# Two relus of batch 1 one chunk later on VectorE, and the last row tile cut as 384 and 128 columns, in a fused linear attention and mixer kernel

## Chip, cores, metric

One core of a Trainium2 chip. The metric is the device time of one launch in microseconds; differences below 1% matter here, so every comparison is between runs of both kernels in the same rounds on the same chip. A profile is one such launch, so it has the scatter of one.

## The reference

Eight batches, 8 heads, 576 positions, head size 64. Linear attention with phi(x) = elu(x) + 1, then a mixer: an MLP over positions (576 to 256 to 576), a residual, an MLP over channels (512 to 1536 to 512), a residual.

```python
q_p, k_p = phi(q), phi(k)
kv  = einsum('bhsd,bhse->bhde', k_p, v);  z = sum(k_p, axis=2)
x   = einsum('bhsd,bhde->bhse', q_p, kv) / (einsum('bhsd,bhd->bhs', q_p, z) + 1e-6)   # heads joined: 512
u   = x + (relu(x.T @ w_tok1) @ w_tok2).T      # mm1, mm2
out = u + relu(u @ w_ch1) @ w_ch2              # mm3, mm4
```

## The kernel before

Everything is in SBUF; the batches are pipelined by hand. A `big` list holds the steps of mm3 and mm4, and after step i the small work of later batches that is listed for i is issued. The order within each engine is the order of issue. The parts that the argument touches (cuts marked `...`):

```python
ps_big = ctx.enter_context(tc.tile_pool(name="ps_big", bufs=4, space=bass.MemoryType.PSUM))
...
def mm3(n, mc, kjs=range(NDM), dve=False):           # chunk mc of 12: 128 hidden channels x 512 positions
    if kjs[0] == 0:
        part_of[mc] = ps_big.tile([128, 512], FP32, name="c_ps", tag="big")
    ...                                              # 4 matmuls (L475)
    if kjs[-1] == NDM - 1 and dve:                   # relu and cast to bf16: VectorE (L479) ...
        nc.vector.tensor_scalar(out=cr[b][:, mc, :], in0=ps, scalar1=0.0, scalar2=None, op0=ALU.max)
    elif kjs[-1] == NDM - 1:                         # ... or ScalarE (L482)
        nc.scalar.activation(out=cr[b][:, mc, :], in_=ps, func=AF.Relu)

def utr_tail_dma(p):                                 # the 9th rows of two batches, transposed by DMA (L464)
    nc.sync.dma_start_transpose(out=uTt, in_=ut[p % 2])

def mm4_last(c):                                     # last row tile of the last batch, in two halves
    p, b, r, cs = B // 2 - 1, 1, R - 1, COLS[c]
    ...                                              # 12 matmuls (L537), add of u on VectorE (L540)
    for e in range(2):
        (nc.scalar if e else nc.sync).dma_start(out=outv[2 * p + b, :, 2 * r + e, cs], in_=o[half[e]])
...
# batch 1: chunks 3..11, then mm3 of the tail rows (three steps), then mm4; phi of k of batch 2 at steps 0 and 2
big = [... mm3(1, mc, range(2, 4)) for mc in range(3)] + [... mm3(1, mc, dve=mc in (4, 7)) for mc in range(3, NCH)] + m3t + ...
fill = [(s, lambda g=g: phi("k", 2, g)) for g, s in ((0, 0), (1, 2))]
fill += [(4, lambda: vcast(2, 0)), (5, lambda: vcast(2, 1, nc.vector.tensor_copy))]
...
# batch 2 (n == 2, d == 1), all on the queue of SyncE: transposes, loads of batch 5, then the tail transpose at step 15
fill += [(12 + d, lambda: qtr_dma(n + 2))]
if n == 2:
    fill += [(12 + d, lambda: load_all(5, "qkv"))]
```

The kernel starts with 27 `warm` matmuls (`warm(27)`) that only keep TensorE busy until the first loads are in.

## Time and profile before

| | |
|---|---|
| time | 266.18 us median of 3 (265.37 to 266.49) |
| span of the profiled run | 264.5 us |
| TensorE busy | 97% |
| last group of matmuls starts, ends | 257.87, 260.65 us |
| from the start of that group to the end of the span | 6.6 us |

With TensorE busy nearly throughout, a time difference must show as a difference in where TensorE stands. A matmul of 512 columns is drawn 0.38 us long but the next one starts 0.216 us later, so up to 0.16 us of standing still can hide between two bars: steps from start to start are the safe measure.

### The profile page before, as it was taken

The numbers are of one execution on the slowest core, as the hardware profiler recorded it, in microseconds if no ns is written. First come the engines' busy times: TensorE is split into PE (matmuls) and PEld (weight loads), VectorE is DVE, ScalarE is ACT, GpSimd is POOL, SyncE is SP. The second block draws the span as 40 slices with busy tenths as digits, with TensorE's granted clock in tenths as the row PEclk, the third lists the DMA queues.
The fourth block names the chain that finished last, engine by engine and source line by source line (L and its number), as shares of the span: only waits on it lengthen the run. The fifth ranks groups of instructions, "written<-read, shape, count | busy, mean of one in ns | idle before, by whom it ended". The sixth has DMA issues, their size and how long they took to land.

```text
span 264.5 us, 5173 instructions
## 1 busy us (share of the span) xinstructions
PE 255.8 (97%) x2119; PEld 135.0 (51%) x2119; DVE 158.3 (60%) x312; ACT 132.8 (50%) x200; POOL 33.0 (12%) x54
## 2 busy tenths in 40 slices
PE   7899999999999999999999999999999999999994
PEld 3585445554744454445564554445554554444643
DVE  5764977966839886948684296938684272420122
ACT  4644878268456358525771358425870354027300
POOL 9720300020002300030001300030001300000000
PEclk9999999999999999999999999999999999999999
DMA  7999999499405997799999991671065500740043
GB/s 249 251 203 276 377 210 400 150 182 402 183 2 105 185 330 283 93 234 347 323 412 216 247 408 54 143 163 45 2 120 131 119 2 0 144 114 2 0 98 101
DMA packets 50087, 48.34 MB, mean 183 GB/s; under 512 B 30288, under 2 KB 35536, under 8 KB 50064
## 3 DMA queue, kind: packets, MB, share of 16 engines
q1 hardware_dynamic: 41904, 35.53, 46.5%
q0 software_dynamic: 7440, 11.44, 20.7%
q10 hardware_dynamic: 720, 1.05, 1.3%
q8 instruction: 16, 0.26, 0.4%
q14 instruction: 7, 0.06, 0.1%
HBM read 35.85 MB, written 9.44 MB: 171 GB/s over the span
## 4 chain that ended last, share of the span: by engine, by line
PE 87%; DVE 5%; DMA 3%; ACT 2%; POOL 1%; issue 1%; ACTq 0%; POOLq 0%
PE h_ps L501 34%; PE c_ps L475 27%; PE a_ps L248 6%; PE h_ps L261 5%; PE c_ps L489 4%; PE nd_ps L210 3%; DMA cr<-in_v_dram 3%; PE kv_ps L169 2%; DVE y L131 1%; PE h_ps L537 1%; DVE cr L479 1%; DVE kp L140 1%; PE bank L363 1%; PE bank L413 1%; DVE e L139 1%
## 5 line engine op out<-in xcount | busy, mean ns | idle before, releaser
L475 PE MATMUL c_ps<-uT,wc 128*128 128x512 bf16 x384 | 91.4, 379 | 0.8 <-ACT uT L444 0.4
L482 ACT ACTIVATE cr<-c_ps 128x512 bf16<-128x512 f32 x91 | 53.5, 599 | 77.1 <-PE c_ps L475 76.9
L501 PE MATMUL h_ps<-wc,cr 128*128 128x512 bf16 x372 | 84.9, 379 | 0.0
L501 PEld LDWEIGHTS <-cr 128*128 128x128 bf16 x372 | 36.0, 98 | 41.3
L475 PEld LDWEIGHTS <-wc 128*128 128x128 bf16 x384 | 35.8, 98 | 37.2 <-issue 1.7
L518 DVE TENSOR_TENSOR o_sb<-h_ps,u 128x512 f32<-128x512 f32 x31 | 21.1, 688 | 23.1 <-PE h_ps L501 23.0
L523 POOL DMA_DIRECT2D out_dram<-o_sb x24 | 14.9, 627 | 154.0 <-DVE o_sb L518 154.0
L222 DVE TENSOR_TENSOR x<-nd_ps,den 128x512 bf16<-128x512 f32 (+1 forms) x42 | 25.3, 602 | 1.4
L139 DVE TENSOR_SCALAR e<-e 128x1152 bf16<-128x1152 bf16 x30 | 13.9, 462 | 12.5 <-ACT e L125 12.4
L273 DVE TENSOR_TENSOR u<-h_ps,x 128x1024 bf16<-128x1024 f32 x12 | 14.3, 1218 | 10.1 <-PE h_ps L261 10.1
L125 ACT ACTIVATE e<-k_raw 128x1152 bf16<-128x1152 f32 x16 | 18.7, 1169 | 2.4 <-DMA k_raw<-in_k_dram 2.4
L125 ACT ACTIVATE e<-q_raw 128x1152 bf16<-128x1152 f32 x16 | 18.5, 1161 | 1.7 <-DMA q_raw<-in_q_dram 1.6
L219 DVE TENSOR_SCALAR den<-nd_ps 128x8 f32<-128x8 f32 (+1 forms) x42 | 6.8, 163 | 19.2 <-PE nd_ps L210 18.5
L261 PE MATMUL h_ps<-ar,w2p 128*128 128x512 bf16 x60 | 16.0, 379 | 0.1
L210 PEld LDWEIGHTS <-qT 128*128 128x128 bf16 x140 | 11.4, 98 | 9.3 <-issue 0.2
L210 PE MATMUL nd_ps<-kvbd,qT 128*128 128x130 bf16 x140 | 15.1, 223 | 0.0
L248 PE MATMUL a_ps<-x,w 128*128 128x512 bf16 x56 | 14.4, 379 | 0.0
L251 ACT ACTIVATE ar<-a_ps 128x512 bf16<-128x512 f32 x14 | 7.6, 594 | 13.2 <-PE a_ps L248 13.2
L528 DVE TENSOR_TENSOR o_sb<-h_ps,ut 128x512 f32<-128x512 f32 x4 | 2.8, 689 | 18.7 <-PE h_ps L501 18.7
L151 ACT CAST vs<-v_raw 128x1152 bf16<-128x1152 f32 x12 | 13.9, 1159 | 0.0
L140 DVE TENSOR_TENSOR qp<-e,y 128x1152 bf16<-128x1152 bf16 x16 | 12.1, 759 | 0.6
L131 DVE TENSOR_SCALAR y<-q_raw 128x1152 bf16<-128x1152 f32 x16 | 12.3, 768 | 0.3
(105 smaller groups left out, 222.4 us busy)
## 6 DMA issues: line engine op xcount, KB each, us to landing
k_raw<-in_k_dram SPq DMA_DIRECT2D x16, 576.0 KB, 9.1
q_raw<-in_q_dram SPq DMA_DIRECT2D x16, 576.0 KB, 7.1
v_raw<-in_v_dram SPq DMA_DIRECT2D x14, 576.0 KB, 10.9
out_dram<-o_sb POOLq DMA_DIRECT2D x24, 256.0 KB, 4.5
wc<-in_moe_w_ch_dram POOLq DMA_DIRECT2D x8, 384.0 KB, 9.9
out_dram<-o_sb SPq DMA_DIRECT2D x9, 128.0 KB, 2.3
out_dram<-o_sb ACTq DMA_DIRECT2D x7, 128.0 KB, 2.6
out_dram<-o_sb POOLq DMA_DIRECT2D x6, 128.0 KB, 7.3
```

The source lines that it names most:

```text
L125: nc.scalar.activation(out=e, in_=f, func=AF.Exp)
L131: nc.vector.tensor_scalar(out=y, in0=f, scalar1=1.0, scalar2=None, op0=ALU.add)
L139: nc.vector.tensor_scalar(out=e, in0=e, scalar1=1.0, scalar2=None, op0=ALU.min)
L210: nc.tensor.matmul(out=o[:, a], lhsT=qT[b][:, t0:t0 + 128], rhs=kvbd[b][:, c, a], start=True, stop=True)
L222: nc.vector.tensor_tensor(out=x[b][:, rs[0]:rs[0] + m, HG * D * g:HG * D * (g + 1)].rearrange("p r (h d) -> p r h d", h=HG), in0=v_[:, :, ...
L248: nc.tensor.matmul(out=ps[:, mt], lhsT=w1t[:, b, ms] if r == R else w1[:, r, ms], rhs=x[b][:, r, :], start=(r == 0), stop=(r == R))
L261: nc.tensor.matmul(out=ps[:, i], lhsT=w2v(kt, r, b), rhs=ar[b][:, kt, :], start=(kt == 0), stop=(kt == NT - 1 and not add))
L475: nc.tensor.matmul(out=ps, lhsT=wc1[:, kj, 128 * mc:128 * mc + 128], rhs=uT[b][:, :, kj], start=(kj == 0), stop=(kj == NDM - 1))
L482: nc.scalar.activation(out=cr[b][:, mc, :], in_=ps, func=AF.Relu)
L501: nc.tensor.matmul(out=ps, lhsT=crt[:, kc, :] if t == 8 else cr[b][:, kc, 128 * r:128 * r + 128], rhs=wc2[:, kc, :], start=(kc == 0), stop ...
L518: nc.vector.tensor_tensor(out=o, in0=ps, in1=u[b][:, r, :], op=ALU.add)
L523: (nc.scalar if last and e else put).dma_start(out=outv[2 * p + b, :, 2 * r0 + e:2 * r0 + e + 2 * m - 1:2], in_=live["o"][half[e], 0:m])
```

## The change

The intent: take off the one TensorE wait for a relu in batch 1 (chunk 4, the fifth product of mm3, is ready near 60 us; VectorE is in phi of k and starts its next relu at 62.16 us only; ScalarE, which has a part of phi too, starts its next one at 60.83 us), and shorten what follows the last matmul.

```diff
-    def mm4_last(c):
-        p, b, r, cs = B // 2 - 1, 1, R - 1, COLS[c]
-        ps = ps_big.tile(...)[:, 0:DM // 2]
+    def mm4_last(cs):
+        p, b, r = B // 2 - 1, 1, R - 1
+        m = cs.stop - cs.start
+        ps = ps_big.tile(...)[:, 0:m]
 ...
-    ... mm3(1, mc, dve=mc in (4, 7)) for mc in range(3, NCH) ...
+    ... mm3(1, mc, dve=mc in (5, 8)) for mc in range(3, NCH) ...
-    fill += [(s, lambda g=g: prep_k(3, g)) for g, s in ((0, 24), (1, 27))]
+    fill += [(s, lambda g=g: prep_k(3, g)) for g, s in ((0, 24), (1, 26))]
-                big = m3(n) + m3t + m4(p, [8, 4, 5, 6]) + [lambda: mm4_last(0), lambda: mm4_last(1)]
+                big = m3(n) + m3t + m4(p, [8, 4, 5, 6]) + [
+                    lambda: mm4_last(slice(0, DM - 128)), lambda: mm4_last(slice(DM - 128, DM))]
```

## The prediction

> **What bounds the kernel now.** I read the page's busy shares first, then the waits of TensorE, then the order of events around the one wait that the change touches, then the last microseconds.
>
> ```profile
> span 264.5 us, 5173 instructions
> PE 255.8 (97%) x2119; PEld 135.0 (51%) x2119; DVE 158.3 (60%) x312; ACT 132.8 (50%) x200; POOL 33.0 (12%) x54
> PE c_ps L475 <- ACT uT L444: 0.4, 1, 0.4
> PE c_ps L475 <- DVE cr L479: 0.4, 1, 0.4
> ```
>
> TensorE (PE) is busy 97% of the span, every other compute engine 60% or less, and the granted clock is 0.999. So time is won only where TensorE stands still. All its waits together come to about 5 us, nearly all in the first 27 us, which the change leaves alone. The last one is the second wait line: a product of mm3 (first channel matmul, L475) waits 0.4 us, once, for a relu on VectorE (L479). The list has no TensorE wait after it. Here are VectorE, ScalarE and TensorE in turn around it (start, duration, engine, what, and in brackets the idle time and what ended it).
>
> ```profile
> 61.49 0.76 DVE L140 TENSOR_TENSOR kp<-e,y 128x1152 bf16<-128x1152 bf16 x1
> 62.16 0.68 DVE L479 TENSOR_SCALAR cr<-c_ps 128x512 bf16<-128x512 f32 x1
> 62.76 0.75 DVE L151 CAST vs<-v_raw 128x1152 bf16<-128x1152 f32 x1
> 63.43 0.68 DVE L479 TENSOR_SCALAR cr<-c_ps 128x512 bf16<-128x512 f32 x1
> 60.83 0.62 ACT L482 ACTIVATE cr<-c_ps 128x512 bf16<-128x512 f32 x1
> 61.31 1.18 ACT L151 CAST vs<-v_raw 128x1152 bf16<-128x1152 f32 x1
> 62.35 1.12 ACT L482 ACTIVATE cr<-c_ps 128x512 bf16<-128x512 f32 x2
> 61.50 0.81 PE L475 MATMUL c_ps<-uT,wc 128*128 128x512 bf16 x3
> 62.14 0.38 PE L475 MATMUL c_ps<-uT,wc 128*128 128x512 bf16 x1
> 62.90 1.02 PE L475 MATMUL c_ps<-uT,wc 128*128 128x512 bf16 x4 [0.38 <-DVE cr L479]
> 63.85 0.32 PE L169 MATMUL kv_ps<-vs,kp 64*64 64x65 bf16 x16
> ```
>
> Number the twelve products of batch 1's mm3 as chunks 0 to 11, four matmuls each. They rotate through four PSUM buffers, so chunk 8 needs the buffer of chunk 4, whose relu is the VectorE one at 62.16. Chunk 4 was complete near 60 us (chunks 5, 6 and 7 follow it, at 0.86 us each, up to 62.4), but VectorE reaches its relu only after the phi of k. It ends at 62.84 and chunk 8 starts at 62.90. The four matmuls of chunk 7 start at 61.50, 61.71, 61.93 and 62.14, so chunk 8 could have started at 62.36: the loss from start to start is 0.54 us. The view says 0.38 because it counts from the modelled end of the last matmul (62.52), which overlaps the next one in steady flow. Chunk 7 itself was held some 0.16 us by ScalarE's relu of chunk 3 (ends 61.45, start 61.50).
>
> **What the Trainium skill says.** "PSUM — Partial Sum Buffer", section "Engine vs sequencer instructions", says that the queues of ScalarE, VectorE and GpSimd are strict first-in first-out; the trace agrees: a relu whose input was ready near 60 us starts at 62.16, right behind phi. "Perfetto Trace Analysis", section "Matmuls", advises rotating independent matmul groups through PSUM banks so that the eviction of one overlaps the next; here four buffers give an eviction about three chunks, 2.6 us, and that one took longer. "TensorE: Matmul & The Clock Gate", section "Wait — 56ns, not 53.3ns?", gives N / 2.4 GHz + 2.5 ns from start to start; chunk 7's steps of 0.21 to 0.22 us at 512 columns agree with its 215.7 ns. "DMA: Bandwidth & Descriptors", section "Specifications", puts the smallest transfer at line rate at 512 B: the new last piece has rows of exactly 128 x 4 = 512 B; no run here shows yet whether that costs.
>
> **The change part by part.** (1) The relus on VectorE are those of chunks 5 and 8 in place of 4 and 7. The compared instruction orders show VectorE's order unchanged (phi of k, relu, cast of v, relu) with a later chunk in each relu, while on ScalarE the relu of chunk 4 comes ahead of the cast of v and that of chunk 8 goes away. Worked out: ScalarE started the cast 0.48 us after relu 3 (61.31 - 60.83), so relu 4 runs from 61.31 to about 61.91. That is before 62.36, so chunk 8 starts at 62.36: **0.54 us saved**. Then chunk 8 issues until 63.22 and kv follows near 63.31 (0.09 us of turn-round, as 63.85 against 63.76 now). Its first half needs the ScalarE cast of v, from 61.79 to 62.97: in time. Its second half starts some 0.35 us later, near 63.66, and needs VectorE's cast, still ending at 63.51: in time by 0.15 us, the thinnest margin of the change. Chunk 9 (at 64.02) needs relu 5, done on VectorE by 62.84; chunk 10 needs relu 6 (from about 62.83 to 63.43). Relu 7 ends near 63.95, before the copy of kv's result to SBUF at about 64.15; relu 8 runs on VectorE from 63.43 to 64.11, before the first denominators. All in time. As TensorE has no listed wait after this, the whole later program should move forward by 0.54 us.
>
> (2) The second half of phi of k for batch 3 is given out one step earlier, behind step 26 in place of 27. No engine's order changes by it: those steps hold no other work for VectorE or ScalarE. **0.**
>
> (3) The end.
>
> ```profile
> 257.87 2.78 PE L537 MATMUL h_ps<-wc,cr 128*128 128x256 bf16 x24
> 259.38 0.42 DVE L540 TENSOR_TENSOR o_sb<-h_ps,u 128x256 f32<-128x256 f32 x1 [0.62 <-PE h_ps L537]
> 260.69 0.42 DVE L540 TENSOR_TENSOR o_sb<-h_ps,u 128x256 f32<-128x256 f32 x1 [0.89 <-PE h_ps L537]
> 259.83 1.78 SPq L542 DMA_DIRECT2D out_dram<-o_sb  x2
> 259.83 1.81 ACTq L542 DMA_DIRECT2D out_dram<-o_sb  x2
> out_dram<-o_sb SPq DMA_DIRECT2D x2, 64.0 KB, 2.0
> out_dram<-o_sb ACTq DMA_DIRECT2D x2, 64.0 KB, 2.3
> ```
>
> The matmuls cost the same in all: 24 x 109 ns now; by the formula 12 x 162.5 + 12 x 55.8 ns, again 2.62 us. The last add shrinks from 0.42 us to about 0.29 (0.69 at 512 columns and 0.42 at 256 give 1.04 ns a column), so it ends 0.13 us earlier. But the larger first piece now ends late: its matmuls near 259.98, its add (about 0.56 us) near 260.58, its issue starts near 260.61. Each issue takes 0.47 us on SyncE and 0.50 on ScalarE, and two back to back on SyncE at 251.01 started 0.52 us apart. So the second issue cannot start before about 261.13, against 261.14 now: the 0.13 us are eaten by the issue of the first piece. What is left is a smaller last transfer: 128 KB land in 2.3 and 2.6 us, 64 KB in 2.0 and 2.3, so 32 KB should take some 0.15 us less; but the first piece, 50% larger and issued 0.8 us later than now, shares the DMA engines with it. I book **0.1 us**, between -0.1 and +0.25.
>
> Sum: 0.54 + 0 + 0.1 = 0.64 us, and 266.18 - 0.64 = 265.54, rounded to 265.5.
>
> **The rivals.** *The wait moves on.* Chunk 9 could wait for relu 5 or kv for the cast of v, and part of the 0.54 us would come back. Against: relu 5 has over 1 us to spare; for: the 0.15 us on the second half of kv, and ScalarE's cast comes 0.48 us later than before. If half of the gain goes, the time is 265.8. *The gain is swallowed later*, by a transfer that keeps its own clock (loads of batches 3 and up, transposes by DMA). Against: no TensorE wait is listed after 63 us; for: waits hidden in the overlap, such as chunk 7's 0.16 us, are not listed. Then 266.1. *The tail turns against the change*: two issues back to back on both queues and 512-byte rows land later than now by 0.3 us; then 265.9. *The tail pays in full*, 0.13 + 0.15 us: 265.4.
>
> **Range and chances.** The three runs before spread over 1.1 us, more than the gain, so a median of three carries about 0.4 us of noise and the start as much again. With 0.2 us for my own sums I take 264.8 to 266.1. A change of 2% is 5.3 us: no part of this can reach that either way, so 0.985 within 2%, and small remainders.
>
> **What would show it.** Right: no wait of mm3 for the relu on VectorE in the changed profile, chunk 8 directly behind chunk 7 at 0.22 us, kv near 63.3, and the end of the last matmul 0.5 us earlier against the start of the span. Last add near 0.29 us, second output issue directly behind the first. Wrong: a new TensorE wait near 63.5 (cast of v) or 64 us; the last matmul earlier by less than 0.4 us; or the stretch from last matmul to end of span, 3.85 us now, growing.

## The result

266.06 us (median of 4, 265.87 to 266.29) against 266.24 us before (median of 4, 265.37 to 266.49). Ratios here are the mean time of one kernel's runs over that of the other's of the same rounds, so not quite the ratio of the medians: 1.000, with a 95% interval of 0.998 to 1.002. A gain of 0.64 us was forecast; 0.18 us of median and nothing of the mean showed. The time lies within the stated range, but the forecast gain was not there, and the two profiled spans are equal, 264.5 us.

In the changed kernel's order of events around chunk 8 (start, duration, engine, what), in order of time:

```profile
57.04 6.79 PE L475 MATMUL c_ps<-uT,wc 128*128 128x512 bf16 x30
...
61.27 1.10 ACT L482 ACTIVATE cr<-c_ps 128x512 bf16<-128x512 f32 x2
...
62.23 1.19 ACT L151 CAST vs<-v_raw 128x1152 bf16<-128x1152 f32 x1
62.60 0.69 DVE L479 TENSOR_SCALAR cr<-c_ps 128x512 bf16<-128x512 f32 x1
63.20 0.75 DVE L151 CAST vs<-v_raw 128x1152 bf16<-128x1152 f32 x1
...
63.76 0.78 PE L169 MATMUL kv_ps<-vs,kp 64*64 64x65 bf16 x72
```

The wait is gone: 30 matmuls run in one piece from 57.04 us, chunk 8 among them, and kv starts 6.72 us after that group's start; before it was 63.85 - 56.60 = 7.25 us. That is 0.53 us saved, as forecast. But the same group started at 57.04 us here and at 56.60 us before: the whole stage came 0.44 us later, from something that happened earlier, in code that the change does not touch. The warm-up and the first kv matmul of batch 0 in the two traces, before and then after:

```profile
1.36 7.46 PE L558 MATMUL bank<-identity 128*128 128x512 bf16 x27 [1.36 <-POOL identity masks.py:199]
...
11.23 0.68 PE L363 MATMUL bank<-cr,kr 64*128 64x128 bf16 x18 [1.02 <-DMA cr<-in_v_dram]
```

```profile
1.36 8.84 PE L559 MATMUL bank<-identity 128*128 128x512 bf16 x27 [1.36 <-POOL identity masks.py:199]
...
11.52 0.68 PE L363 MATMUL bank<-cr,kr 64*128 64x128 bf16 x18
```

Before, kv had to wait for the load of v; after, kv stood behind a warm-up that took 1.4 us longer, and started 0.29 us later. The other 0.15 us of the 0.44 were lost near 35 us: the transposes of q of batch 1 (L180) waited 0.95 us for VectorE there, 0.61 us before. "TensorE: Matmul & The Clock Gate", section "Part 1: The HAM clock gate", says that the array runs at half rate until a free-running activity window of some 3.4 us has been busy, so that the changeover depends on where in the window a run starts. The traces agree that there are two rates and that the changeover moves: 512-column matmuls start 0.43 us apart until about 4.3 us in the one and 6.9 us in the other, and about 0.22 us apart after it. How far it moves differs from the page's 500 ns to either side, as the two are 2.6 us apart; the 7 and 13 slow steps here fit its other statement, 6, 11 or 14 slow matmuls from run to run of one kernel.

The end of the changed kernel:

```profile
257.80 2.78 PE L538 MATMUL h_ps<-wc,cr 128*128 128x384 bf16 x24
259.95 0.96 DVE L541 TENSOR_TENSOR o_sb<-h_ps,u 128x384 f32<-128x384 f32 x2 [1.26 <-PE h_ps L538]
260.54 0.47 SPq L543 DMA_DIRECT2D out_dram<-o_sb  x1
260.55 0.50 ACTq L543 DMA_DIRECT2D out_dram<-o_sb  x1
261.10 0.55 SPq L543 DMA_DIRECT2D out_dram<-o_sb  x1
261.14 0.79 ACTq L543 DMA_DIRECT2D out_dram<-o_sb  x1
```

The last add ends at 259.95 + 0.96 = 260.91 us, 0.20 us earlier than before. The last issues start at 261.10 and 261.14 us; before, both started at 261.14 us. They stand behind the issues of the first piece (260.54 and 260.55 us in the lines above), as forecast: the add had ended 0.19 us before.

The two spans can now be added up, in us, after minus before: start of mm3 of batch 1 +0.44 (55.52 - 55.08); chunk 8 -0.54; a denominator step near 119 us that took 0.12 longer, seen in this one trace only and not followed further; a wait near 131 us that was 0.10 before and 0 after (below); from the last row tile to the end +0.07 (6.70 - 6.63, from spans that are given to 0.1 us only). Sum -0.01, and the spans are equal to that accuracy.

### The profile page after: what moved, and what is told of

Same layout as the page of the kernel before. It is cut to its first block, busy times and chain, and to the rows that moved or that the text cites. A ratio compares the mean times of both kernels' runs of the same rounds, so it can differ in the third digit from the quotient of the medians.

```text
span 264.5 us, 5155 instructions
## 1 busy us (share of the span) xinstructions
PE 255.8 (97%) x2101; PEld 134.9 (51%) x2119; DVE 159.0 (60%) x312; ACT 132.7 (50%) x200; POOL 33.0 (12%) x54
## 4 chain that ended last, share of the span: by engine, by line
PE 92%; DVE 4%; ACT 1%; issue 1%; POOL 0%; ACTq 0%; POOLq 0%
PE h_ps L501 34%; PE c_ps L475 29%; PE a_ps L248 5%; PE h_ps L261 5%; PE c_ps L489 4%; PE bank L559 4%; PE nd_ps L210 3%; PE kv_ps L169 2%; DVE y L131 1%; PE h_ps L538 1%; PE bank L363 1%; PE bank L413 1%; DVE cr L479 1%; DVE kp L140 1%; DVE e L139 1%
## 5 line engine op out<-in xcount | busy, mean ns | idle before, releaser
L139 DVE TENSOR_SCALAR e<-e 128x1152 bf16<-128x1152 bf16 x30 | 14.3, 477 | 12.2 <-ACT e L125 12.1
L273 DVE TENSOR_TENSOR u<-h_ps,x 128x1024 bf16<-128x1024 f32 x12 | 14.3, 1219 | 10.1 <-PE h_ps L261 10.1
L140 DVE TENSOR_TENSOR qp<-e,y 128x1152 bf16<-128x1152 bf16 x16 | 12.1, 759 | 0.6
```

The costliest lines, as they stand in the source:

```text
L139: nc.vector.tensor_scalar(out=e, in0=e, scalar1=1.0, scalar2=None, op0=ALU.min)
```

## The experiments

Two theories stood at the start. A: the 0.54 us are real, and a scattering start hid them. B: they are given back somewhere between chunk 8 and the end. The three rounds ran on three chips, each with its own runs of the kernel before. In every trace I measured the same distances: the first kv matmul of batch 0 (when v is in), the first mm3 matmul of batch 1, and the stretch from there to the start of the last row tile. All fourteen traces, with the wait near 131 us that the second round of experiments is about:

| kernel | first kv | first mm3, batch 1 | stretch | wait at mm3's tail | stretch less wait |
|---|---|---|---|---|---|
| before | 11.23 | 55.08 | 202.79 | 0.10 | 202.69 |
| before_again | 11.01 | 54.86 | 203.01 | 0.32 | 202.69 |
| tail_only | 11.12 | 54.97 | 202.91 | 0.22 | 202.69 |
| after | 11.52 | 55.52 | 202.28 | 0 | 202.28 |
| after_again | 10.40 | 54.26 | 202.34 | 0.20 | 202.14 |
| after_third | 10.68 | 54.53 | 202.61 | 0.46 | 202.15 |
| relu_only | 11.18 | 55.03 | 202.80 | 0.65 | 202.15 |
| relu_only_2 | 11.32 | 55.18 | 202.30 | 0.15 | 202.15 |
| warm20 | 11.04 | 54.89 | 202.27 | 0.11 | 202.16 |
| before_utt_first | 11.07 | 54.92 | 202.70 | 0 | 202.70 |
| after_utt_first | 10.91 | 54.77 | 202.16 | 0 | 202.16 |
| tail320 | 10.33 | 54.18 | 202.16 | 0 | 202.16 |
| best_again | 11.35 | 55.21 | 202.15 | 0 | 202.15 |
| v0_early | 10.14 | 57.97 | 202.15 | 0 | 202.15 |

The wait is the step from the first mm2 matmul ahead of mm3's tail to the first tail matmul, less the 0.86 us (four matmuls at 0.216) that it takes where nothing holds it.

### First round: the parts by themselves, 5 rounds each

**after_again**: the changed kernel, unaltered.

> The changed kernel again, unaltered, to separate a small gain from scatter. Theory A (the 0.53 us at the eighth chunk of mm3 are real, and were hidden by a start that scatters with the warm-up matmuls and the first loads): mean of the fast runs 0.3 to 0.6 us below the kernel before; in the trace, from the first mm3 matmul of batch 1 (the group of 6 near 55 us) to the start of the last row tile's second-layer matmuls 202.28 us again, against 202.79 in the kernel before. Theory B (the gain is given back somewhere between): that stretch is 202.6 us or more, and the times are equal to within 0.15 us.

265.3 us median (6 runs, 264.76 to 266.31), before 266.18 (11 runs); ratio 0.9974 (0.9958 to 0.999). So the changed kernel is faster after all, by about 0.7 us here; its trace has the earliest start of the three of this kernel (54.26 us).

**relu_only**: `dve=mc in (4, 7)` to `(5, 8)` in the kernel before, nothing else.

> The kernel before with only the two relus moved from chunks 4 and 7 to chunks 5 and 8. Theory A: 0.4 to 0.6 us less than before, and 0 to 0.1 us less than the changed kernel, because the new tail gives nothing. Stretch from first mm3 matmul of batch 1 to the start of the last row tile 202.3 us. Theory B: within 0.15 us of before.

265.94 us (5 runs), ratio 0.9993 (0.9982 to 1.0005): a miss for theory A. And in its trace the stretch is 202.80 us, as if chunk 8 had gained nothing, though kv came 8.24 us after the first mm3 matmul (before: 8.77). So in this run 0.54 us were indeed given back later, as theory B says. Comparing the starts of each stage shows where: 0.59 us ahead of the kernel before at the last mm1 matmul ahead of it (127 us), 0.05 us at 145 us. In between:

```profile
129.63 1.03 PE L261 MATMUL h_ps<-ar,w2p 128*128 128x512 bf16 x4
131.14 1.05 PE L489 MATMUL c_ps<-uTt,wc 128*128 128x128 bf16 x16 [0.48 <-DMA uTt<-ut]
```

The first matmul of mm3's tail waits for `uTt`, the tail rows of batches 2 and 3, transposed by DMA: 131.14 - 129.63 - 0.86 = 0.65 us. The same place in the kernel before, in the chain of work that ended last (start, duration, what), has a trace of it:

```profile
131.24 0.99 PE c_ps L489 x16
...
133.10 1.79 PE c_ps L489 x32
```

Sixteen tail matmuls take 0.99 us in the first piece, where two pieces together take 1.79, that is 0.89 each: 0.10 us of waiting that no list of waits shows, because the bars overlap. The transpose lands with no time to spare, so whatever brings TensorE there earlier may have to wait. Why it lands so late is in SyncE's queue, kernel before:

```profile
113.85 2.30 SPq L112 DMA_DIRECT2D q_raw<-in_q_dram  x2
116.25 1.91 SPq L112 DMA_DIRECT2D k_raw<-in_k_dram  x2
118.21 1.80 SPq L112 DMA_DIRECT2D v_raw<-in_v_dram  x2
120.14 3.61 SPq L464 DMA_TRANSPOSE uTt<-ut  x1
```

Six loads of 576 KB for batch 5 (3.5 MB) are queued just ahead of it, and the transpose lands 11.0 us after its issue, at 131.1 us. "DMA: Bandwidth & Descriptors", section "Queues, rings and completion order", says that an engine consumes the descriptors of a ring in order, which would put the transpose behind all six loads; the next round tests it.

**tail_only**: the kernel before with only the last row tile cut as 384 and 128.

> The kernel before with only the last row tile split as 384 and 128 columns. Theory A (the second issue stands behind the first on its engine, so the shorter last add gains nothing): from the end of the last matmul to the end of the span 3.85 to 3.95 us, as against 3.85 before and 3.92 after; the time equal to before within 0.15 us. Rival C (the tail is what cost the gain): 0.2 to 0.5 us slower than before, with the stretch after the last matmul above 4.1 us. Stretch of mm3 as before, 202.8 us.

266.22 us, ratio 0.9997 (0.9984 to 1.0011). The add ends earlier, but the issues start 3.30 and 3.34 us after the start of the last row tile (before: 3.27); from the start of that tile to the end of the span it is 6.6 us, as before, and 3.8 us of it come after the last matmul. In the trace the tail gives nothing and takes nothing. The interval of the ratio alone would allow 0.4 us less or 0.3 us more; it is the trace that rules out rival C.

**warm20**: the changed kernel with `warm(20)`.

> The changed kernel with 20 warm-up matmuls in place of 27. Theory A says that the start scatters because the 27 warm-up matmuls took 7.46 us in the one trace and 8.84 us in the other, at the slow rate for a different number of them, and that in the second they held the first q transposes back to 10.04 us, past what the first loads set. With 20 they end by 8.7 us even in the slow case (14 at 0.43 us, 6 at 0.22 us), so the first q transposes start at 8.4 to 8.8 us, the first mm3 matmul of batch 1 at 55.1 us or earlier, and the time is 0.1 to 0.4 us below the changed kernel, with a smaller spread. Rival D (start set by the loads alone): no difference from the changed kernel. Rival E: the clock falls back in the gap and the start is later by over 0.5 us.

265.76 us, ratio 0.9991 (0.9971 to 1.0012), and runs from 264.91 to 267.05. A miss: 0.1 to 0.4 us below the changed kernel was expected, and its mean of 265.95 us is 0.5 us above that of after_again in the same rounds, with a wider spread. My assumption was off too: the 20 took 7.30 us, because most of them ran at the slow rate. The first q transposes did start early (8.50 us), but kv then waited 0.99 us for v (11.04 us). What the trace does show: the start has two limits, the warm-up and the load of v, and taking away one leaves the other. Rival E is not excluded: the slowest run (267.05 us) has a mean granted clock of 0.991, the other five 0.998 to 1.000. That run has no trace, so where its clock fell isn't known.

### Second round: the queue, the start and the end

**after_utt_first** and **before_utt_first**: the loads of batch 5 queued behind the transpose instead of ahead of it, in the changed kernel and in the kernel before. The loads have time: they are used a batch later.

```diff
-                fill += [(12 + d, lambda: load_all(5, "qkv"))]
+                fill += [(15, lambda: load_all(5, "qkv"))]
```

> The changed kernel, with the loads of batch 5 queued on SyncE behind the transpose of the joined tail rows (uTt) of batches 2 and 3 in place of ahead of it. Theory F (the gain was there at chunk 8, and part of it is lost again near 130 us, where mm3's tail waits for that transpose, which lands 10.8 to 12.1 us after its issue because 3.5 MB of loads are queued ahead of it; in five of the six traces so far it lands 0.1 to 0.65 us too late): the transpose lands within 5 us of its issue, no wait at mm3's tail, and the stretch from the first mm3 matmul of batch 1 to the start of the last row tile is 202.15 us (before: 202.79; relus alone: 202.80). Time 0.5 to 0.9 us below the kernel before. Theory A alone (only the start scatters): stretch 202.3 us as in the changed kernel, no help from this edit.

> The kernel before with the same reordering of the loads behind the transpose. Theory F: stretch 202.69 us (the 0.54 us at chunk 8 are still in it, the 0.10 us at mm3's tail are gone); time 0 to 0.3 us below before, and 0.54 us above the changed kernel with the same reordering, in the same rounds. If the relus are worth less than the traces say, the two differ by less than 0.3 us.

The transpose landed 5.5 and 5.3 us after its issue (expected: within 5), and TensorE no longer waits. Changed kernel with the reordering:

```profile
112.81 2.16 SPq L464 DMA_TRANSPOSE uTt<-ut  x1
...
129.38 1.03 PE L261 MATMUL h_ps<-ar,w2p 128*128 128x512 bf16 x4
130.24 1.06 PE L489 MATMUL c_ps<-uTt,wc 128*128 128x128 bf16 x16
```

The tail starts 0.86 us after mm2, four steps of a matmul. The transpose was also issued 6 to 7 us earlier, because issuing the six loads had taken SyncE over 6 us (113.85 to 120.14 us above). So the loads ahead of it are shown as the cause of the late landing; whether it stood behind them in the ring or shared the DMA engines with them is not told apart. The stretches are 202.16 and 202.70 us, both as expected to 0.01, and 0.54 us apart: with the transpose out of the way, the moved relus are worth what was forecast. The times in the same rounds: 265.78 us (ratio 0.9977, 0.9954 to 1.0; one run at 267.2) and 266.27 us (0.9991, 0.9973 to 1.001), 0.49 us apart in the medians and 0.31 us in the means.

**v0_early**: after_utt_first with the load of v of batch 0 ahead of GpSimd's memsets.

```diff
+    for c in range(2):
+        load_v0(c)
     nc.gpsimd.memset(w1t, 0.0)
     nc.gpsimd.memset(qT[0], 0.0)
     nc.vector.memset(qT[1], 0.0)
-    for c in range(2):
-        load_v0(c)
```

> The changed kernel with the reordered loads, and with the loads of v of batch 0 issued by GpSimd ahead of its two memsets (0.5 and 2.0 us) in place of behind them. Theory G (in all traces the first mm3 matmul of batch 1 comes 43.85 to 44.00 us after the first kv matmul of batch 0, and that one starts at 10.40 to 11.52 us, when v of batch 0 lands or the warm-up ends, so this is where the scatter of the total sits): first kv matmul at 10.0 to 10.5 us, and 0.3 to 0.9 us less than the changed kernel with reordered loads. Rival: the loads of k and q share the DMA engines and come later in turn, so nothing is gained or some 0.3 us are lost.

267.41 us, ratio 1.0029 (0.9996 to 1.0062). The first kv matmul came at 10.14 us, as expected, but the second loads of q and k came later in turn (their exps start at 9.71 and 12.96 us; before 8.28 and 10.26), and mm3 of batch 1 started at 57.97 us. That fits the rival (what v gains, k and q lose), but it is not all: this trace has a granted clock of 0.51 from 14.7 to 18.0 us. Against after_utt_first TensorE is 1.93 us later when the waits for the late q and k are over (14.74 us, where the other has 12.81), and it loses another 1.26 us up to 18.21 us, in that stretch of low clock. The record has the same split: three of the six runs have a mean clock of 0.991 to 0.994 and took 267.88 to 268.97 us; the three at 1.000 took 266.32 to 266.94 us, mean 266.58, where after_utt_first has a mean of 266.01. So at full clock the kernel is 0.6 us slower than after_utt_first, as the rival says, and the runs with a low clock are another 1.3 to 2.4 us slower. Why the clock fell was not tested. Theory G holds for the scatter only: in twelve of the other thirteen traces the first mm3 matmul of batch 1 comes 43.85 or 43.86 us after the first kv matmul, so all the start's scatter, 10.33 to 11.52 us, is there by then (the changed kernel's first trace has 44.00).

**tail320**: after_utt_first with the last row tile as 320 and 192 columns.

```diff
-                    lambda: mm4_last(slice(0, DM - 128)), lambda: mm4_last(slice(DM - 128, DM))]
+                    lambda: mm4_last(slice(0, DM - 192)), lambda: mm4_last(slice(DM - 192, DM))]
```

> The changed kernel with the reordered loads and the last row tile as 320 and 192 columns in place of 384 and 128. If the issue of the first piece is what eats the shorter last add: first issue near 260.15 us on the changed kernel's scale, second issue at the end of the second add and not behind the first, 0.06 to 0.10 us earlier after the last matmul than with 384 and 128 (2.06 us instead of about 2.12 us after the last matmul group of 2.78 us... that is, 3.21 us after that group's start in place of 3.30 us). Total equal to the changed kernel with reordered loads within 0.2 us. If the bytes of the last transfer set the end instead: 0.05 to 0.1 us slower.

```profile
256.34 2.78 PE L538 MATMUL h_ps<-wc,cr 128*128 128x320 bf16 x24
258.17 0.49 DVE L541 TENSOR_TENSOR o_sb<-h_ps,u 128x320 f32<-128x320 f32 x1 [0.94 <-PE h_ps L538]
259.16 0.36 DVE L541 TENSOR_TENSOR o_sb<-h_ps,u 128x192 f32<-128x192 f32 x1 [0.50 <-PE h_ps L538]
259.55 0.47 SPq L543 DMA_DIRECT2D out_dram<-o_sb  x1
259.55 0.53 ACTq L543 DMA_DIRECT2D out_dram<-o_sb  x1
```

The second issue now follows its add (259.16 + 0.36 = 259.52) and not the first issue: 3.21 us after the start of the last row tile, as expected, against 3.30 and 3.34. From the start of that tile to the end of the span it is 6.5 us, against 6.6 to 6.7 in the traces of the other two cuts. So the issue of the first piece was what ate the shorter add. 265.56 us, ratio 0.9963 (0.994 to 0.9986); 0.22 us below after_utt_first in the medians, where at most 0.2 either way was expected.

### Third round: does the wait belong to the moved relus?

Up to here the wait at mm3's tail was 0.10 and 0.22 us without the moved relus and 0 to 0.65 with them. Four kernels, 5 rounds, to tell scatter from a systematic loss; the fourth is tail320 again, under the name **best_again**.

> The kernel before, unaltered, for a second trace of it. Theory F: stretch from the first mm3 matmul of batch 1 to the last row tile 202.69 us plus what mm3's tail waits for the transpose of the tail rows (0.10 and 0.22 us in the two traces of this schedule so far), so 202.7 to 203.0 us. Time equal to the other runs of before within scatter.

> The changed kernel a third time. Stretch 202.15 us plus the wait at mm3's tail, which was 0, 0.20, 0.65 and 0.11 us in the four traces of kernels with the moved relus. If that wait scatters by itself, 0 to 0.3 us is likely, and the mean time is 0.2 to 0.6 us below before; if the earlier schedule makes it systematically longer (the transpose keeping its own clock), 0.3 to 0.65 us and a time within 0.2 us of before.

> The kernel with the moved relus alone, again: it was the one trace with a long wait (0.65 us) at mm3's tail and gained only 0.19 us in the mean. If the wait scatters: 0 to 0.3 us this time, time 0.2 to 0.6 us below before. If it belongs to this schedule: 0.5 us or more again, time within 0.2 us of before.

> The changed kernel with reordered loads and 320 and 192 columns in the last row tile, again, as the candidate that beats both. Stretch 202.15 us with no wait at mm3's tail, and 6.4 to 6.5 us from the start of the last row tile to the end of the span (6.6 to 6.7 in all others): 0.7 to 1.0 us below before, and 0.2 to 0.5 us below the changed kernel.

before_again: 266.28 us, ratio 0.9994 (0.9977 to 1.0012), wait 0.32 us, so a stretch of 203.01. It is the same program as the kernel before, whose median in these rounds is 266.42, so a difference of 0.14 us means nothing here. after_third: 265.72 us, ratio 0.9978 (0.996 to 0.9997), wait 0.46. relu_only_2: 265.63 us, ratio 0.9971 (0.9953 to 0.9988), wait 0.15. So relu_only's 0.65 us and its small gain did not come back with the same program. With the moved relus the wait was 0, 0.11, 0.15, 0.20, 0.46 and 0.65 us (mean 0.26); without them 0.10, 0.22 and 0.32 (mean 0.21). It scatters, and so few traces show no systematic loss; they don't exclude one of 0.1 or 0.2 us. after_third's longer wait lies in the range that I had named for a systematic loss while its time lies in that of scatter, so by itself that run decides nothing.

best_again: 265.27 us, ratio 0.9957 (0.9938 to 0.9976); 0.45 us below after_third of the same rounds in the medians and 1.15 us below before, more than the 0.7 to 1.0 us expected. This version beats the kernel before, and the changed kernel in the one round that had both.

## Why the prediction was right or wrong

In short: the mechanism at chunk 8 was right and worth its 0.54 us. What failed is the step from there to the total, "Sum: 0.54 + 0 + 0.1 = 0.64 us": its term for the end measured 0, it has no term for the start, which came 0.44 us later in the profiled pair, and the 0.54 us do not reach the end of the program in every run.

- **The wait at chunk 8, 0.54 us.** Right. The stretch less the wait at the tail is 202.69 or 202.70 us in all four traces without the moved relus, and 202.14 to 202.16 us in all with them but the first (202.28, with the unexplained 0.12 us). The checks on kv, the cast of v and relus 5 to 8 held: no new wait there.
- **"As TensorE has no listed wait after this, the whole later program should move forward by 0.54 us."** This step failed for single runs. At mm3's tail TensorE meets a transpose that lands 0 to 0.65 us too late, and there the gain is kept or lost from run to run. I had named such a wait as a rival ("The gain is swallowed later") and had the sign of it in hand, 0.99 us where 0.89 is usual, but looked in the list of waits, which does not show waits that fit under the overlap of two matmuls. In relu_only's profiled run it took all of the gain. In the changed kernel's own first profile it took nothing, so it is not what hid the gain there; and on the average the wait is 0.26 us with the moved relus and 0.21 without, so a loss in every run is not shown.
- **What hid the gain in the first comparison.** In the profiled pair it was the start: 0.44 us later, 0.29 of it by the warm-up and the load of v. The prediction set the start aside as what "the change leaves alone" and counted its scatter only in the range, not against the gain; in the three traces of the changed kernel alone mm3 of batch 1 starts at 54.26 to 55.52 us. Its reading that nearly all waits lie in the first 27 us was loose as well: 0.61 us at 34.93 and 0.24 us each at 52.20 and 53.69 come later, and the first of these grew to 0.95 us in the changed kernel's first trace. For the runs that were not profiled the cause stays open. The changed kernel's three sets gave ratios of 1.000, 0.9974 and 0.9978; the mean of its 15 runs is 265.70 us, that of the 24 runs of before in the same rounds 266.23: 0.53 us, pooled over three rounds on three chips, where 0.64 was forecast and the first comparison had nothing of the mean. I had put 0.4 us on a median; with a gain of that size four runs against four could not decide, and the forecast of a clear gain in them was too bold.
- **The earlier phi of k for batch 3, 0.** Right so far as can be seen: no engine's order changed. It was not run alone, but after_third and relu_only_2, which differ by it and by the tail, are 0.09 us apart.
- **The end, 0.1 us.** Wrong by its whole size: 0, with and without the relus. The mechanism was right (the second issue stands behind the first), but that second issue started 3.30 and 3.34 us after the tile's start instead of the forecast 3.26, took longer itself (0.55 and 0.79 us instead of 0.47 and 0.50), and the smaller last transfer landed 2.0 and 2.2 us after it started, where I counted on 0.15 less than 2.0 and 2.3. Whether its 512-byte rows cost anything can't be told apart from the slower issue; the 48 KB of tail320's last piece, in rows of 768 bytes, landed in 1.8 and 2.1 us. Moving the cut to 320 turned it into a gain of about 0.15 us.

Open: what makes the transpose land early or late from run to run, the start of the runs without a trace, the drop of the clock in v0_early, and the 0.12 us near 119 us in one trace.

## What to carry to other kernels

When a stall is taken away on the bounding engine, follow that engine to the end and ask of each later input how early it lands, not whether a wait for it is listed: a stage that takes 0.1 us longer than its twin is a wait that hides under overlapping bars. A small transfer on the critical path belongs ahead of bulk loads that are not yet needed. And where the expected gain is about the spread of single runs, compare distances between fixed events inside the traces, which here agreed to 0.01 us, and count on more than four runs for the total.

## What the Trainium skill lacked or had wrong

- "TensorE: Matmul & The Clock Gate" (section "Seeing it yourself"): it warns that the clock events of a trace are unreliable, but not that they can miss the slow start altogether. The granted clock that the profile shows for the first 8 us was 1.00 in both kernels, while 512-column matmuls started 0.43 us apart until 4.3 and 6.9 us; that column can't be used to see the warm-up (27 matmuls in 7.4 to 8.8 us, 20 in 7.3 us in the one trace of them). It did show the later drop to 0.51 in v0_early.
- "Perfetto Trace Analysis": it says that the end of a matmul is estimated and not measured, but not how much waiting that hides: bars of 0.38 us follow each other at 0.216 us here, waits of 0.10 and 0.22 us at mm3's tail were in no list of waits, and 0.65 us was listed as 0.48.
- "DMA: Bandwidth & Descriptors": no figure for what a queued transfer loses to those ahead of it; a transpose of the tail rows landed 10.1 to 12.1 us after its issue behind 3.5 MB of loads, 5.1 to 5.5 us ahead of them.
- The same page (section "Issuing engines are not separate DMA queues") says that the time to issue a transfer is usually small beside the transfer. Here two stores in a row on one queue started 0.56 to 0.60 us apart (SyncE and ScalarE), and the second issue took 0.55 and 0.79 us instead of 0.47 and 0.50, of 2.0 and 2.2 us to landing. That ate a VectorE saving of 0.13 us.
